# Forgetting attention, then a gelu MLP, on one core: the tail tile of v multiplied apart, the opening's normalisation reordered, and the output units of the steps spread anew

## The chip, the cores and the metric

The kernel runs on one core of one Trainium2 chip. The metric is device time in microseconds from one launch. Before the change the median of three runs is 338.88 us (338.82 to 339.25).

TensorE (PE in the profile) multiplies matrices; VectorE (DVE), ScalarE (ACT) and GpSimd (POOL) work on elements; SyncE (SP) and POOL issue the transfers of this kernel. Each engine takes its instructions in the order in which the kernel writes them.

## The reference, cut to what matters

Attention over 8 batches of 8 heads, 576 positions and head width 64, with a decay built from the running sum of log f and a causal mask; then an MLP with tanh-gelu on all 8 x 576 = 4608 tokens, 512 to 2048 to 512.

```python
scores = scale * np.matmul(q, k.transpose(0, 1, 3, 2))
log_f = np.log(np.clip(f, 0.0001, 1.0))
cum = np.cumsum(log_f, axis=-1)
decay = cum[:, :, :, None] - cum[:, :, None, :]
scores = np.where(causal, -1000000000.0, scores + decay)
attn = exp(scores - max) / (sum + 1e-09)
x = (attn @ v) as [4608, 512]
h = x @ w_in
g = 0.5 * h * (1.0 + np.tanh(c * (h + 0.044715 * h * h * h)))
return g @ w_out
```

The row's own part of the decay cancels between numerator and denominator. What is left is a weight per key, w = exp(-cum), which the kernel multiplies into v and uses again, in bf16, as the vector that gives the denominators.

## The kernel before, in words

Four heads of one batch are a *quad*; two quads make a batch, 16 quads in all. For a quad the kernel

- reorders q and k on DVE (`transpose_qk`, two instructions, line 142);
- multiplies v by the key weights into `vw` (`make_vw`, line 152). v lies in `v_nat` as five tiles of up to 128 keys. The fifth, slot `TAIL` = 4, holds the last 64 keys in its upper half, zeros in the lower. A sixth slot of `vw`, `HEAD`, repeats the first 64 keys. So `make_vw` issues two instructions: 128 x 1280 elements (five tiles of four heads of 64) and 64 x 256;
- computes scores in three rounds (`score_round`: line 170 on PE, then two exps on ACT, line 201, into `pt`), masks them on POOL (line 226);
- multiplies `pt` with the weights for the denominators (line 247, w_bf), takes reciprocals with two DVE transposes around them (lines 278 to 282), multiplies `pt` with `vw` for the outputs, two halves y = 0, 1, and scales each half into `xT` (`normalise`, line 288).

The MLP runs in chunks of 512 tokens. `mlp_in(j)` multiplies `xT` by w_in in eight pairs of psum banks, each followed by a gelu on ACT (line 329). `mlp_out(j)` is a generator: each pull emits one *unit*, one of the 16 matmuls that accumulate an output tile of 128 tokens (line 356). Four tiles of 16 units are 64 units per chunk. After the sixteenth unit DVE copies the tile out of psum (line 361) and SP stores it. A unit is one matmul with 128 columns of weights, or four with 32 columns each where the neighbours use 32 columns as well. Two psum banks (`psM`) hold the tiles.

The opening (`startup`) treats batch 0 apart. Its quads 0 and 1 use only the first 512 queries (`early_rounds`, `early_product`), which don't need the tail tile; the last 64 queries of both quads come later together (`late_scores`, `late_denominators`, `late_outputs`), and only these read slot `TAIL` of `vw`. SP loads v of quad 0 in five transfers, the tail last; POOL loads v of quad 1, then w_in in four transfers, q and k of quad 2, w_out in four, q and k of quad 3, v of batch 1. DVE's order in the opening is: transposes of quads 0 and 1, `w_bf`, `vw` of quad 0, reciprocals of quad 0, `vw` of quad 1, two normalisations of quad 0, reciprocals of quad 1, two normalisations of quad 1. The banks of the early products come from a pool of two (`psP`), so the denominators of quad 1 take the bank that the first half of quad 0's outputs had.

Then come the *steps*. `step(i, j, fill, fills)` runs three rounds r = 0, 1, 2. Each has a score round of quad i, a product of quad j (denominators, then the two halves of the outputs), and `fills[r]` units of the output of the chunk before; the transposes of the next quad, the masks and `make_vw` are placed in rounds by hand. Score banks are two pairs (tag "s"), so round r + 1 reuses the banks that the exps of round r read. In batch 0 six units are pulled first, then steps 2, 3 and 4 follow with 28, 14 and 11 units, 59 in all. The last five are drained after the first pair of the next `mlp_in`. In the batches after that two steps per batch run with units in the same way: `pull(fill, 6)`, then 26 and 27 units, again five left over.

The order is written by hand (`manual_schedule`); no planner moves anything.

Of the kernel before, what the change touches and what calls it, by code (L numbers as in the profile page):

```python
# [16 lines left out]
def kernel(  # L17
# [10 lines left out]
    nc = tc.nc  # L28

    B, H, S, D = q.shape  # L30
    BH = B * H
    NT = (S + 127) // 128
# [6 lines left out]
    NQ = BH // 4  # L39
    QPB = H // 4  # L40
# [6 lines left out]
    TAIL, HEAD = NT - 1, NT  # L47
# [25 lines left out]
    def many(n, shape, dtype, name):  # L73
        return [singles.tile(shape, dtype, name=f"{name}{i}") for i in range(n)]
# [6 lines left out]
    v_nat = many(2, [128, NT, H, D], FP32, "v_nat")  # L81
# [3 lines left out]
    vw = many(2, [128, NT + 1, 4, D], BF16, "vw")  # L85
# [8 lines left out]
    wT = singles.tile([128, NQ, NT, 4], FP32, name="wT")  # L94
# [15 lines left out]
    def load_qk(i):  # L110
        b, h0 = i // QPB, 4 * (i % QPB)
        return [nc.gpsimd.dma_start(  # L112
            out=dst[i % 2].rearrange("p a d -> p (a d)"),
            in_=src[b, h0:h0 + 4].rearrange("h (p a) d -> (h p) (a d)", p=32))
            for src, dst in ((k, k_c), (q, q_c))]
# [30 lines left out]
                    .rearrange("p (a d) -> p a d", d=D // 2),  # L146
            )

    def make_vw(i, eng=nc.gpsimd):
        h0 = 4 * (i % QPB)  # L150
        for p, n, slot in ((128, NT, 0), (64, 1, HEAD)):
            eng.tensor_mul(  # L152
                vw[i % 2][:p, slot:slot + n], v_nat[(i // QPB) % 2][:p, 0:n, h0:h0 + 4, :],
                wT[:p, i, 0:n, :].unsqueeze(3).to_broadcast([p, n, 4, D]))

    def bank_pair(tag, name):
        return pools[tag].tile([128, 2, 512], FP32, name=name, tag=tag)
# [1 line left out]
    def make_lows():  # L159
        for low, parts in zip(lows, (diag_first, diag)):  # L160
            nc.gpsimd.memset(low, 0.0)
            for p0, p1, pattern in parts:
                nc.gpsimd.affine_select(
                    out=low[p0:p1, :], in_=low[p0:p1, :], compare_op=ALU.is_ge, fill=-32768.0,
                    base=0, pattern=pattern, channel_multiplier=-1)
# [92 lines left out]
    def early_product(i, groups, ps):  # L258
        product(i, groups, ps, 0, early_parts, (0,))
        return ps  # L260
# [25 lines left out]
    def normalise(i, y, po):  # L286
        n, t0 = po.shape[-1], S * (i // QPB) % RING
        nc.vector.tensor_mul(xT[:, 2 * (i % QPB) + y, t0:t0 + n], po, rbs[i][:, 0:n])  # L288
# [87 lines left out]
    def startup():  # L376
        nc.sync.dma_start(out=f_sb, in_=f.rearrange("b h s -> (b h) s"))
        q0 = load_qk(0)[1]
        make_identity(nc, ident_f32)
        k1 = load_qk(1)[0]  # L380
        make_identity(nc, ident)
        make_lows()

        nc.vector.memset(blank, 0.0)
        warm = pools["p"].tile([128, 512], FP32, name="warm", tag="p")
        warm_up(warm, 11)
        nc.vector.memset(ones_f32, 1.0)
        nc.vector.memset(shift, -64.0)
        nc.vector.memset(wT[:128 - LAST, :, TAIL, :], 0.0)
        nc.vector.memset(w_bf[LAST:, :, HEAD, :], 0.0)  # L390
        for t_ in vw:
            nc.vector.memset(t_[LAST:, HEAD, :, :], 0.0)
        for t_ in v_nat:
            nc.vector.memset(t_[:128 - LAST, TAIL, :, :], 0.0)
        nc.vector.tensor_scalar(f_sb, f_sb, 1e-4, 1.0, op0=ALU.max, op1=ALU.min)
        nc.scalar.activation(f_sb, f_sb, AF.Ln)
        nc.vector.tensor_tensor_scan(cum_sb, ones_f32, f_sb, 0.0, op0=ALU.mult, op1=ALU.add)
        cum = pools["p"].tile([128, 512], FP32, name="small", tag="p")[:, 0:NT * BH]
        for t in range(NT):
            s0 = min(128 * t, S - 128)  # L400
            nc.tensor.transpose(cum[:, t * BH:(t + 1) * BH],
                                cum_sb[:, s0:s0 + 128], ident_f32)
        make_w(cum)
        warm_up(warm, 6)
        transpose_qk(0)
        transpose_qk(1)
        nc.vector.tensor_copy(w_bf[:, :, :NT, :], wT)
        nc.vector.tensor_copy(w_bf[:LAST, :, HEAD, :], wT[:LAST, :, 0, :])
        after(load_v(0, heads=slice(0, 4))[0], q0)
        make_vw(0, nc.vector)  # L410
        after(load_v(0, nc.gpsimd, slice(4, 8))[0], k1)
        for c in range(2):
            for u in range(QPB):
                load_w_in(c, u)
        load_qk(2)
        for c in range(4):
            load_w_out(c)
        q3 = load_qk(3)[1]
        load_v(1, nc.gpsimd, slice(0, 4))
        after(load_v(1, heads=slice(4, 8))[0], q3)  # L420

        def single(name):
            return pools["p"].tile([128, 512], FP32, name=name, tag="p")

        for r, tags, n in ((0, ("s", "s"), 4), (1, ("x", "s"), 4), (2, ("s", "x"), 2)):
            score_round(0, r, tags, True)
            warm_up(warm, n)
        score_round(1, 0, ("s", "s"), True)
        reciprocals(0, early_product(0, den_groups(0), single("po")))
        make_vw(1, nc.vector)  # L430
        score_round(1, 1, ("x", "s"), True)
        nums = [early_product(0, out_groups(0, y), single("po")) for y in range(2)]
        for y in range(2):
            normalise(0, y, nums[y])
        score_round(1, 2, ("s", "x"), True)
        late_scores()
        reciprocals(1, early_product(1, den_groups(1), single("po")))
        po = bank_pair("x", "po")
        nums = [early_product(1, out_groups(1, y), po[:, y, :]) for y in range(2)]
        phs = [bank_pair("s", "ps_h") for _ in range(2)]  # L440
        for dts in ((0, 1), (2,), (3,)):
            for ft in range(4):
                mlp_mm(0, ft, phs[ft // 2][:, ft % 2, :], dts)
            if dts[0] == 0:
                for y in range(2):
                    normalise(1, y, nums[y])
        for u in range(2):
            gelu(0, u, phs[u])
        for u in range(2, N_FT // 2):
            mlp_in(0, (u,), "x" if u % 3 == 2 else "s")  # L450
# [10 lines left out]
    def step(i, j, fill, fills):  # L461
        for r in range(3):
            if i is not None:
                score_round(i, r)
            if j is not None:
                if r == 0:
                    denominators(j)
                else:
                    attn_out(j, r - 1, "s" if i is None and r == 1 else "po")
            if (i, r) in ((2, 0), (3, 1)):  # L470
                transpose_qk(i + 1)
            if i is not None and r > 0:
                mask(i, r - 1)
            if i is not None and r == {2: 2, 3: 1}.get(i, 0):
                make_vw(i, nc.vector if i == 2 else nc.gpsimd)
            pull(fill, fills[r], 128 if j is None else 32)
            if i is not None and r == 2:
                mask(i, 2)
                if i == 2:
                    load_v(2)  # L480
                elif i < 5:
                    load_qk(i + 2)
# [9 lines left out]
    with tc.manual_schedule():  # L492
        with psum("psX", 1) as pools["x"], psum("psP", 2) as pools["p"]:
            startup()
            prepare(2)
        pools["po"] = ctx.enter_context(psum("psO", 1))
        pools["m"] = ctx.enter_context(psum("psM", 2))
        fill = none
        for b in range(B):
            if b > 0:  # L500
                mlp_in(b, (0,))
                for x in fill:
                    pass
                prepare(2 * b + 3, 2 * b + 4)
                if b + 2 < B:
                    load_v(b + 2)
                mlp_in(b, range(1, N_FT // 2))
            if b + 1 < B:

                nc.scalar.activation(scrap, shift, AF.Exp)  # L510
            fill = mlp_out(b)
            if b == 0:
                late_denominators(bank_pair("po", "po")[:, 0, :])
                pull(fill, 6, 32)
                late_outputs(bank_pair("po", "po")[:, 0, :])
                step(2, None, fill, (12, 8, 8))
                step(3, 2, fill, (4, 5, 5))
                step(4, 3, fill, (4, 4, 3))
            elif b + 1 < B:
                i = 2 * b + 3  # L520
                pull(fill, 6)
                step(i, i - 1, fill, (9, 8, 9))
                step(i + 1 if i + 1 < NQ else None, i, fill, (9, 8, 10))
        mlp_in(B, range(N_FT // 2))
        for j in (B - 1, B):
            for x in mlp_out(j):
                pass
# [30 lines left out]
```

## Time and profile before

| | |
|---|---|
| median of three runs | 338.88 us |
| the profiled execution's own time | 338.56 us |
| its span, first to last instruction | 336.9 us |
| PE busy | 328.6 us, 98% of the span |
| ACT busy | 191.3 us, 57% |
| DVE busy | 124.1 us, 37% |
| POOL busy | 115.3 us, 34% |
| granted TensorE clock | 1.000 |

A row of the timeline gives the start in us from the span's start, the length of the merged group, the engine, the line of the kernel, the operation with output and input tiles and shapes, the count, and in brackets the idle time before it with what ended it. PEld is the weight load, which overlaps the matmuls; SPq and POOLq are the engines' issuing of transfers. A group counts as busy from its first start to its last end, so a wait in its middle can hide in it. In a row on transfers the last number is the time from issue to landing.

### The profile page before, as it was taken

The page shows a single profiled execution, that of the slowest core. Times are in us where ns is not written, and L with a number is a line of the kernel's source. Part 1 is how long each engine was busy: PE and PEld are TensorE (multiplying, and loading weights), DVE is VectorE, ACT ScalarE, POOL GpSimd, SP SyncE. Part 2 cuts the span into 40 slices and gives each one's busy share as a digit, 9 for nine tenths or more (in the row PEclk, how much of TensorE's full clock was granted, in tenths as well). Part 3 has the DMA queues.
Part 4 walks back from the last instruction along what each step waited for, and adds up shares of the span by engine and source line. Part 5 has one row for each costly group of instructions (what it writes and reads, how often), then busy time and mean ns, then how long its engine had stood idle before and what let it go on. Part 6 is the DMA issues. An engine that isn't in the chain of part 4 may idle for free.

```text
span 336.9 us, 9983 instructions
## 1 busy us (share of the span) xinstructions
PE 328.6 (98%) x4513; PEld 161.0 (48%) x4535; DVE 124.1 (37%) x172; ACT 191.3 (57%) x206; POOL 115.3 (34%) x159
## 2 busy tenths in 40 slices
PE   7989999999999999999999999999999999999996
PEld 2554534444444444444478444444444454444444
DVE  7582177342526144604442342524330450000121
ACT  4876766767565757467555756576647704553000
POOL 6933248751534145242725162405520300000000
PEclk9999999999999999999999999999999999999999
DMA  7999999597107801491129310921000010000112
GB/s 130 210 188 210 220 241 204 83 221 144 66 33 156 157 33 66 95 207 44 35 71 207 73 65 33 186 57 66 34 33 0 35 64 31 2 0 27 68 69 86
DMA packets 45578, 33.29 MB, mean 99 GB/s; under 512 B 34304, under 2 KB 34560, under 8 KB 45536
## 3 DMA queue, kind: packets, MB, share of 16 engines
q0 software_dynamic: 7232, 14.81, 24.6%
q1 hardware_dynamic: 38304, 17.85, 19.9%
q8 instruction: 35, 0.57, 0.7%
q14 instruction: 7, 0.06, 0.1%
HBM read 36.85 MB, written 9.44 MB: 137 GB/s over the span
## 4 chain that ended last, share of the span: by engine, by line
PE 89%; DMA 3%; issue 3%; ACT 1%; DVE 1%; SPq 1%; POOL 1%; POOLq 0%; DVEq 0%; ACTq 0%
PE ps_h L320 37%; PE pso L356 35%; PE po L247 9%; PE ps_s L170 7%; DMA v_nat<-in_v_dram 2%; DMA q_c<-in_q_dram 1%; ACT pt L201 1%; DVE vw L152 1%; SPq L118 1%; POOL pt L226 0%; POOLq L553 0%; DVE den L278 0%; DVE xT L288 0%; POOL k_c L112 0%; DVE o_st L361 0%
## 5 line engine op out<-in xcount | busy, mean ns | idle before, releaser
L356 PE MATMUL pso<-w_out_sb,gT 128*32 128x512 bf16 (+2 forms) x1633 | 133.6, 377 | 0.5 <-issue 0.3
L320 PE MATMUL ps_h<-xT,w_in_sb 128*128 128x512 bf16 (+1 forms) x625 | 126.1, 357 | 0.9 <-issue 0.2
L201 ACT ACTIVATE pt<-ps_s 128x1024 bf16<-128x1024 f32 (+1 forms) x96 | 91.1, 1002 | 41.1 <-PE ps_s L170 37.9
L329 ACT ACTIVATE gT<-ps_h 128x1024 bf16<-128x1024 f32 (+1 forms) x81 | 74.1, 928 | 70.4 <-PE ps_h L320 69.7
L320 PEld LDWEIGHTS <-w_in_sb 128*128 128x128 bf16 x640 | 62.0, 98 | 63.5 <-issue 3.3
L356 PEld LDWEIGHTS <-gT 128*32 128x32 bf16 (+1 forms) x1639 | 59.7, 97 | 55.1 <-issue 0.8
L226 POOL TENSOR_SCALAR_AFFINE_SELECT pt<-pt 128x512 bf16<-128x512 bf16 (+1 forms) x70 | 44.1, 638 | 103.3 <-ACT pt L201 102.2
L361 DVE COPY o_st<-pso 128x512 f32<-128x512 f32 (+1 forms) x37 | 25.0, 675 | 88.0 <-PE pso L356 88.0
L278 DVE STREAM_TRANSPOSE den<-po 128x576 f32<-128x576 f32 (+2 forms) x17 | 12.7, 748 | 70.3 <-PE po L247 65.2
L152 POOL TENSOR_TENSOR vw<-v_nat,wT 128x1280 bf16<-128x1280 f32 (+1 forms) x26 | 37.7, 1471 | 0.5 <-DVE rec L280 0.4
L288 DVE TENSOR_TENSOR xT<-po,rb 128x576 bf16<-128x576 f32 (+1 forms) x32 | 23.8, 748 | 34.8 <-PE po L247 34.7
L170 PE MATMUL ps_s<-qT,kT 32*128 32x64 bf16 (+8 forms) x944 | 34.0, 286 | 1.4 <-ACT pt L201 1.1
L247 PE MATMUL po<-pt,vw 128*32 128x64 bf16 (+6 forms) x768 | 27.5, 277 | 0.0
L170 PEld LDWEIGHTS <-kT 32*128 32x128 bf16 (+1 forms) x944 | 14.7, 97 | 25.3 <-issue 21.9
L142 DVE STREAM_TRANSPOSE kT<-k_c 128x576 f32<-128x576 f32 x16 | 20.0, 1247 | 8.8 <-DMA k_c<-in_k_dram 8.8
L247 PEld LDWEIGHTS <-vw 128*32 128x32 bf16 x832 | 13.7, 96 | 13.7 <-issue 7.1
L142 DVE STREAM_TRANSPOSE qT<-q_c 128x576 f32<-128x576 f32 x16 | 19.9, 1241 | 0.8 <-DMA q_c<-in_q_dram 0.8
L112 POOL DMA_DIRECT2D k_c<-in_k_dram x16 | 9.1, 568 | 29.3 <-DVE kT L142 22.7
L247 PE MATMUL po<-pt,w_bf 128*32 128x64 bf16 (+8 forms) x384 | 14.3, 276 | 0.5 <-DVE xT L288 0.5
L282 DVE STREAM_TRANSPOSE rb<-rec 128x576 f32<-128x576 f32 (+2 forms) x17 | 12.6, 743 | 0.6
L112 POOL DMA_DIRECT2D q_c<-in_q_dram x16 | 8.7, 545 | 8.7 <-DVE qT L142 5.1
L329 ACT ACT_TABLE_LOAD x8 | 10.3, 1283 | 0.1
(43 smaller groups left out, 72.6 us busy)
## 6 DMA issues: line engine op xcount, KB each, us to landing
out_dram<-o_st SPq DMA_DIRECT2D x35, 256.0 KB, 2.1
v_nat<-in_v_dram SPq DMA_DIRECT2D x24, 256.0 KB, 6.3
k_c<-in_k_dram POOLq DMA_DIRECT2D x16, 288.0 KB, 6.1
q_c<-in_q_dram POOLq DMA_DIRECT2D x16, 288.0 KB, 7.3
w_in_sb<-in_moe_w_in_dram POOLq DMA_DIRECT2D x4, 512.0 KB, 9.8
w_out_sb<-in_moe_w_out_dram POOLq DMA_DIRECT2D x4, 512.0 KB, 17.9
v_nat<-in_v_dram SPq DMA_DIRECT2D x14, 128.0 KB, 5.6
v_nat<-in_v_dram POOLq DMA_DIRECT2D x8, 128.0 KB, 7.2
```

The lines of the kernel that those rows point to most:

```text
L112: return [nc.gpsimd.dma_start(out=dst[i % 2].rearrange("p a d -> p (a d)"), in_=src[b, h0:h0 + 4].rearrange("h (p a) d -> (h p) (a d)", p=32))
L142: nc.vector.transpose(out=dst[i % 2].rearrange("p s c -> p (s c)").bitcast(FP32) .rearrange("p (t a) -> p a t", a=S // 32), in_=src[i % 2] ...
L152: eng.tensor_mul(vw[i % 2][:p, slot:slot + n], v_nat[(i // QPB) % 2][:p, 0:n, h0:h0 + 4, :], wT[:p, i, 0:n, :].unsqueeze(3).to_broadcast([ ...
L170: nc.tensor.matmul(tiles[h // 2][m0:m0 + m, h % 2, c0:c0 + nq], kT[i % 2][32 * h:32 * h + 32, k0:k0 + m, c], qT[i % 2][32 * h:32 * h + 32, ...
L201: nc.scalar.activation(pt[i % 2][:, 2 * g:2 * g + 2, off:off + n], tiles[g][:, :, 0:n], AF.Exp, scale=scale)
L226: nc.gpsimd.affine_select(out=p[p0:p1, :, o:o + 128], in_=p[p0:p1, :, o:o + 128], compare_op=ALU.is_ge, fill=0.0, base=0, pattern=[[0, 4]] ...
L247: nc.tensor.matmul(ps[r0:r0 + w.shape[-1], o:o + nq], w, rhs[:, h, col:col + nq], start=(n in fresh), stop=(n in (0, len(parts) - 1)), ski ...
L288: nc.vector.tensor_mul(xT[:, 2 * (i % QPB) + y, t0:t0 + n], po, rbs[i][:, 0:n])
L320: nc.tensor.matmul(ph[:, o:o + m], w[:, dt], xT[:, dt, a:a + m], start=(dt == 0 and o == 0), stop=(dt == N_DT - 1), skip_group_check=True)
L329: nc.scalar.activation(gT[:, 2 * u + y:2 * u + y + n, o:o + CHUNK], ph[:, y:y + n, :], AF.Gelu_apprx_tanh)
L356: nc.tensor.matmul(ps[m:m + w, c0:c1], gT[:, ft, c + m:c + m + w], w_out_sb[:, ft, c0:c1], start=(ft == 0), stop=(ft == N_FT - 1), skip_gr ...
L361: nc.vector.tensor_copy(st[:, c0:c1], ps[:, c0:c1])
```

## The change

The diff does five things. `make_vw` takes a range of tiles; the opening calls it without the tail for both quads, and once more for the tail of each behind the normalisations of quad 1. `vw` of quad 1 is made after the normalisations of quad 0 and after the scores of its second round are written, not before. The transposes of quad 3 move from round 0 to round 1 of step 2. The units of steps 2, 3 and 4 become 26, 15 and 17, so that with the six ahead all 64 are pulled and none is left over. In the last batch that has steps, the last step takes 32 units instead of 27, again with none left over.

```diff
-    def make_vw(i, eng=nc.gpsimd):
+    def make_vw(i, eng=nc.gpsimd, t0=0, t1=NT):
         h0 = 4 * (i % QPB)
-        for p, n, slot in ((128, NT, 0), (64, 1, HEAD)):
-            eng.tensor_mul(
-                vw[i % 2][:p, slot:slot + n], v_nat[(i // QPB) % 2][:p, 0:n, h0:h0 + 4, :],
-                wT[:p, i, 0:n, :].unsqueeze(3).to_broadcast([p, n, 4, D]))
+        for p, a, z, slot in ((128, t0, t1, t0), (64, 0, 1, HEAD)):
+            if a >= t0:
+                eng.tensor_mul(
+                    vw[i % 2][:p, slot:slot + z - a],
+                    v_nat[(i // QPB) % 2][:p, a:z, h0:h0 + 4, :],
+                    wT[:p, i, a:z, :].unsqueeze(3).to_broadcast([p, z - a, 4, D]))
...
         after(load_v(0, heads=slice(0, 4))[0], q0)
-        make_vw(0, nc.vector)
+        make_vw(0, nc.vector, 0, TAIL)
...
         reciprocals(0, early_product(0, den_groups(0), single("po")))
-        make_vw(1, nc.vector)
         score_round(1, 1, ("x", "s"), True)
         nums = [early_product(0, out_groups(0, y), single("po")) for y in range(2)]
         for y in range(2):
             normalise(0, y, nums[y])
+        make_vw(1, nc.vector, 0, TAIL)
         score_round(1, 2, ("s", "x"), True)
         late_scores()
...
                 for y in range(2):
                     normalise(1, y, nums[y])
+        for i in range(QPB):
+            make_vw(i, nc.vector, TAIL)
         for u in range(2):
             gelu(0, u, phs[u])
...
-            if (i, r) in ((2, 0), (3, 1)):
+            if (i, r) in ((2, 1), (3, 1)):
                 transpose_qk(i + 1)
...
-                step(2, None, fill, (12, 8, 8))
-                step(3, 2, fill, (4, 5, 5))
-                step(4, 3, fill, (4, 4, 3))
+                step(2, None, fill, (10, 8, 8))
+                step(3, 2, fill, (4, 6, 5))
+                step(4, 3, fill, (6, 6, 5))
...
                 step(i, i - 1, fill, (9, 8, 9))
-                step(i + 1 if i + 1 < NQ else None, i, fill, (9, 8, 10))
+                if i + 1 < NQ:
+                    step(i + 1, i, fill, (9, 8, 10))
+                else:
+                    step(None, i, fill, (9, 9, 14))
```

## The prediction

> **What bounds the kernel now.** I read the page's busy line, then the order of time in the opening and in steps 2 to 4 (PE, DVE and ACT apart), then the chain of waits, then single transfers.
>
> ```profile
> span 336.9 us, 9983 instructions
> PE 328.6 (98%) x4513; PEld 161.0 (48%) x4535; DVE 124.1 (37%) x172; ACT 191.3 (57%) x206; POOL 115.3 (34%) x159
> ```
>
> PE is the bound, and an edit that only moves its work gains nothing where PE streams without a gap. It can gain where PE waits: visibly, or hidden in groups that take longer than the same group elsewhere. The change touches two such places. The first is the opening, in order of time, DVE and then PE:
>
> ```profile
> 14.89 1.82 DVE L152 TENSOR_TENSOR vw<-v_nat,wT 128x1280 bf16<-128x1280 f32 x2 [2.54 <-DMA v_nat<-in_v_dram]
> 16.63 0.70 DVE L278 STREAM_TRANSPOSE den<-po 128x512 f32<-128x512 f32 x1
> 17.65 0.71 DVE L282 STREAM_TRANSPOSE rb<-rec 128x512 f32<-128x512 f32 x1
> 18.29 1.78 DVE L152 TENSOR_TENSOR vw<-v_nat,wT 128x1280 bf16<-128x1280 f32 x2
> 19.99 1.27 DVE L288 TENSOR_TENSOR xT<-po,rb 128x512 bf16<-128x512 f32 x2
> ...
> 14.89 0.73 PE L247 MATMUL po<-pt,w_bf 128*32 128x64 bf16 x20
> ...
> 17.08 1.28 PE L247 MATMUL po<-pt,vw 128*32 128x64 bf16 x40
> ...
> 19.60 0.66 PE L170 MATMUL ps_s<-qT,kT 32*128 32x64 bf16 x62 [0.44 <-ACT pt L201]
> 20.72 0.73 PE L247 MATMUL po<-pt,w_bf 128*32 128x64 bf16 x20 [0.46 <-DVE xT L288]
> 21.26 1.28 PE L247 MATMUL po<-pt,vw 128*32 128x64 bf16 x40
> ```
>
> DVE is one queue here: vw of quad 0, the reciprocals of quad 0, vw of quad 1, the two normalisations of quad 0. PE's denominators of quad 1 need a bank that the first normalisation frees; they wait 0.46 us for it.
>
> The second place is steps 3 and 4, PE and then ACT:
>
> ```profile
> 47.14 0.91 PE L170 MATMUL ps_s<-qT,kT 32*64 32x512 bf16 x24
> 52.61 0.88 PE L170 MATMUL ps_s<-qT,kT 32*128 32x320 bf16 x16
> 58.30 0.63 PE L170 MATMUL ps_s<-qT,kT 32*128 32x64 bf16 x14 [0.25 <-ACT pt L201]
> 61.00 0.63 PE L170 MATMUL ps_s<-qT,kT 32*128 32x320 bf16 x14 [0.17 <-ACT pt L201]
> 63.00 1.90 PE L320 MATMUL ps_h<-xT,w_in_sb 128*128 128x512 bf16 x7
> 64.74 1.24 PE L356 MATMUL pso<-w_out_sb,gT 128*128 128x512 bf16 x5
> ...
> 50.87 1.94 ACT L201 ACTIVATE pt<-ps_s 128x1024 bf16<-128x1024 f32 x2 [0.76 <-PE ps_s L170]
> 53.52 1.94 ACT L201 ACTIVATE pt<-ps_s 128x1024 bf16<-128x1024 f32 x2 [0.70 <-PE ps_s L170]
> 56.31 1.94 ACT L201 ACTIVATE pt<-ps_s 128x1024 bf16<-128x1024 f32 x2 [0.86 <-PE ps_s L170]
> ...
> 63.63 1.28 ACT L329 ACT_TABLE_LOAD   x1
> 64.94 1.02 ACT L329 ACTIVATE gT<-ps_h 128x1024 bf16<-128x1024 f32 x1
> ```
>
> Each round is scores, a product, and some fill units of the out tile before. Six rounds take 47.14 to 63.00, 15.86 us. What PE itself needs for a round is seen where nothing waits, in the chain of waits of the next batch (start, length, what):
>
> ```profile
> 79.37 0.59 PE ps_s L170 x16
> ...
> 80.75 1.94 PE pso L356 x36
> 82.70 0.57 PE ps_s L170 x16
> ...
> 85.79 0.57 PE ps_s L170 x16
> ```
>
> A round with 9 units (36 matmuls) takes 82.70 - 79.37 = 3.33 us, one with 8 takes 3.09; a unit is 1.94/9 = 0.2155, so a round without units costs 1.37 to 1.39. The six rounds hold 25 units, so PE needs 6 x 1.38 + 25 x 0.2155 = 13.7 us, and 2.2 us are waits, most of them inside groups that count as busy (0.88 for scores that take 0.57 there). ACT sets the pace: its pairs of exps start 2.65 to 2.79 us apart (50.87, 53.52, 56.31), 1.94 of work and 0.7 to 0.86 from the end of the second exp through the scores that reuse its bank to the next first exp. A round of n units on PE is 1.38 + 0.2155 n: 2.24 for 4, 2.46 for 5, 2.67 for 6. Up to six units fit.
>
> **The change part by part.** *Opening.* Durations first, from the groups by form, then the chain's rows for the loads of v and the landing of the fourth of them:
>
> ```profile
> L152 DVE TENSOR_TENSOR vw<-v_nat,wT 128x1280 bf16<-128x1280 f32 x3 | 4.4, 1478 | 3.0 <-DMA v_nat<-in_v_dram 3.0
> L152 DVE TENSOR_TENSOR vw<-v_nat,wT 64x256 bf16<-64x256 f32 x3 | 1.2, 407 | 0.0
> 8.49 0.51 SPq L118
> 9.04 5.72 DMA v_nat<-in_v_dram
> v_nat<-in_v_dram SPq DMA_DIRECT2D x1, 128.0 KB, 4.5
> ```
>
> (1478 - 407)/1024 is 1.046 ns per element, so 1024 elements take 1.21 us, and the pair, which overlapped by 0.07, 1.55 instead of 1.82. Without the tail, vw of quad 0 waits for the fourth load, 8.49 + 4.5 = 12.99, not for 9.04 + 5.72 = 14.76: it runs from about 13.1 to 14.7. The reciprocals then wait for PE's denominators (14.89 + 0.73 = 15.62) and, with 1.73 as now (16.63 to 18.36), end near 17.4. The normalisations now follow at once: the first half of PE's outputs is there at 17.08 + 0.73 = 17.81, so they run 17.9 to 19.15. Then vw of quad 1, to 20.70. PE finishes the late scores at 20.26 (they still wait for ACT), starts the denominators there instead of at 20.72, and the outputs 0.54 later, at 20.80; vw of quad 1 is ready 0.1 before. Gain 0.46 us. That is the top of this term, since ACT's wait ahead of it stays; if vw of quad 0 still began at 14.89, the same sum puts vw of quad 1 at 21.0 and leaves 0.26; the bottom is 0. I take 0.46, since every term is a row of this stretch.
>
> The two tail multiplications are new: 0.41 each by the row of equal width, behind the normalisations of quad 1. DVE is idle there:
>
> ```profile
> 29.54 1.26 DVE L142 STREAM_TRANSPOSE kT<-k_c 128x576 f32<-128x576 f32 x1 [4.90 <-DMA k_c<-in_k_dram]
> ```
>
> They fit in those 4.90 us, and their reader, the late outputs, comes only behind the whole first MLP. Cost nothing; without that cover, 0.8.
>
> *What the earlier PE runs into.* The last quarter of w_out serves units 13 to 16 of the first out tile. Six units run before step 2, so it is first read by the seventh of step 2:
>
> ```profile
> 22.38 0.71 POOL L135 DMA_DIRECT2D w_out_sb<-in_moe_w_out_dram  x1 [1.81 <-DMA w_in_sb<-in_moe_w_in_dram]
> w_out_sb<-in_moe_w_out_dram POOLq DMA_DIRECT2D x1, 512.0 KB, 17.9
> 39.56 2.54 PE L356 MATMUL pso<-w_out_sb,gT 128*128 128x512 bf16 x11 [0.16 <-issue]
> ```
>
> It lands at 22.38 + 17.9 = 40.28 and is read at 39.56 + 6 x 0.2155 = 40.85 now, at 40.39 then; with 0.13 from landing to start (14.76 to 14.89 above) that is a tie. Cost 0 to 0.3, I take 0.05.
>
> *Step 2, (12,8,8) to (10,8,8).* Its later rounds are at ACT's pace too, so two units fewer in the first bring everything behind forward by 0.43. *Step 3, (4,5,5) to (4,6,5), and step 4, (4,4,3) to (6,6,5).* Seven units more. Five of them go into rounds that have room: 0 to 0.1 each for the three rounds of six, where PE's 2.67 meets ACT's 2.65; I take 0.1 in all, 0.3 is the end. The two in the last round have no exp behind them to hide under: +0.43. In return the five left over between the first and second pair of the next MLP, 5 x 0.2155 = 1.08 at 64.74, are gone. Steps together: 0.43 - 0.1 - 0.43 + 1.08 = 0.98 gained, bounds 0.78 and 1.08, and 0 if the long groups were work.
>
> What those five covered: the gelu table. All is early by 0.46 + 0.43 = 0.89 there: the load begins at 63.63 - 0.89 = 62.74 and ends at 64.02, the first pair of the MLP ends near 64.4, its gelu (1.02) near 65.6, and the third pair wants that bank near 66.1, a pair of eight matmuls (8 x 0.2155) later: 0.5 to spare. The gelu starts at 64.94, 0.03 after its load ended at 64.91, so nothing stands between them. [...]
>
> *Transposes of quad 3, a round later.* They wait for their load anyway:
>
> ```profile
> 42.43 1.26 DVE L142 STREAM_TRANSPOSE kT<-k_c 128x576 f32<-128x576 f32 x1 [3.12 <-DMA k_c<-in_k_dram]
> 43.53 1.24 DVE L142 STREAM_TRANSPOSE qT<-q_c 128x576 f32<-128x576 f32 x1
> ```
>
> They end at 44.77 in either place; step 3's first scores come at 47.14 - 0.89 = 46.25. Ahead of them DVE now copies out tile 0, which it had to hold back; behind them stand vw of quad 2, which waits for its load until 45.76 (row below), and the second copy. No DMA moves with them. Nothing gained, nothing lost. *Last batch, (9,8,10) to (9,9,14):* PE streams there at 0.2155 a unit before and after; 0.
>
> **Sum.** 0.46 - 0.05 + 0.98 = 1.4 us. The profiled execution took 338.56 us (span 336.9 and 1.66 around it) and becomes 337.16; the median shown, 338.88, stands 0.32 above it, so 337.5.
>
> **The rivals.** *Steps only, 337.9:* the late quarter of w_out, or vw of quad 1 missing its 0.1, eats the opening's gain. For it: both margins are a tenth. Against: each must miss by 0.4 to take all. *Opening only, 338.4:* PE's long groups are work, not waiting, and the fill is paid in full. Against it: the same groups take 0.57 in the next batch. *The tail is not parted, 337.7:* if the wait follows the whole tile and not its slots, vw of quad 0 still starts at 14.89; the opening gives 0.26, the sum 1.2. Against it: vw of quad 2 started when half the heads of its tile were still being issued.
>
> ```profile
> 44.80 3.37 SPq L118 DMA_DIRECT2D v_nat<-in_v_dram  x2
> ...
> 45.76 1.82 DVE L152 TENSOR_TENSOR vw<-v_nat,wT 128x1280 bf16<-128x1280 f32 x2 [0.48 <-DMA v_nat<-in_v_dram]
> ```
>
> *The gelu table uncovered, 337.7:* if a load's length again (1.28) passes before a gelu can start, the first gelu ends at 64.02 + 1.28 + 1.02 = 66.3, the third pair waits 0.2, and the sum is 1.2; the 0.03 us is against it. [...]
>
> *Slower, 339.9:* the loads on POOL's queue come one slot later. One slot is about 2.5 us (the wait of 1.81 and the issue of 0.71 in the row at 22.38). The place is unit 13 of the first out tile: PE waits there in order, and all the margin, 0.57 before, is spent by the earlier PE. From 1.4 us late it decides; one slot costs 2.45: 338.9 - 1.4 + 2.45. Against it: nothing in the opening's DMA order is changed.
>
> **How the numbers follow.** Forecast 0.60, steps only 0.13, opening only 0.09, tail not parted 0.05, table 0.03, slower 0.10. About 0.2%, 0.68 us, is what a measurement of this kernel tells from no change. The forecast, steps only, the tail and the table lie beyond it, but for some 0.06 of the weight at their weak ends: faster 0.75; opening only and those ends: same 0.15; slower 0.10. Terms at their best give 0.46 + 1.08 = 1.54, and 0.4 for what rows of one execution leave open: 336.9. The upper end reaches to opening only and a little past it, 338.7.
>
> **What would show it.** Right: vw with 1024 elements starting near 13.1, no wait for normalisation before the denominators of quad 1, the outputs of quad 1 at 20.8 and not 21.26; no out units after the next MLP's first pair, the second pair near 64.4 instead of 64.74 + 1.08 = 65.82; scores of steps 3 and 4 at ACT's pace as before. Wrong: PE waiting for w_out near 40.4, outputs of quad 1 waiting for vw near 20.8, exps of steps 3 and 4 more than 2.8 us apart, the third MLP pair waiting for a gelu.

## The result, and the profile after

| | before | after |
|---|---|---|
| median | 338.74 us (9 runs, 338.49 to 339.25) | 337.88 us (9 runs, 337.60 to 338.67) |
| the profiled execution | 338.56 us | 338.67 us |
| its span | 336.9 us | 337.0 us |

The ratio is 0.9976, 95% interval 0.9965 to 0.9986: 0.86 us faster, where 1.4 was forecast (337.5, range 336.9 to 338.7). The profiled execution of the changed kernel is the longest of its nine, and longer than the profiled one of before. That turns out to be useful: it shows the place where the executions differ.

The page of the changed kernel, busy times (PE's share fell, at a longer span):

```profile
span 337.0 us, 10056 instructions
PE 327.8 (97%) x4549; PEld 160.8 (48%) x4571; DVE 124.8 (37%) x174; ACT 191.3 (57%) x206; POOL 115.1 (34%) x159
```

Its opening in order of time, DVE and then PE:

```profile
13.19 1.55 DVE L154 TENSOR_TENSOR vw<-v_nat,wT 128x1024 bf16<-128x1024 f32 x2 [0.78 <-DMA v_nat<-in_v_dram]
17.73 1.29 DVE L291 TENSOR_TENSOR xT<-po,rb 128x512 bf16<-128x512 f32 x2 [0.43 <-PE po L250]
18.93 1.54 DVE L154 TENSOR_TENSOR vw<-v_nat,wT 128x1024 bf16<-128x1024 f32 x2
...
23.90 0.75 DVE L154 TENSOR_TENSOR vw<-v_nat,wT 128x256 bf16<-128x256 f32 x2
...
19.46 0.66 PE L173 MATMUL ps_s<-qT,kT 32*128 32x64 bf16 x62 [0.44 <-ACT pt L204]
20.05 0.73 PE L250 MATMUL po<-pt,w_bf 128*32 128x64 bf16 x20
20.61 1.26 PE L250 MATMUL po<-pt,vw 128*32 128x64 bf16 x40
21.81 1.69 PE L323 MATMUL ps_h<-xT,w_in_sb 128*128 128x512 bf16 x6
25.04 2.33 PE L323 MATMUL ps_h<-xT,w_in_sb 128*128 128x512 bf16 x10 [1.54 <-issue]
```

In this execution everything up to the first MLP is as forecast: vw waits for its own load alone, the denominators of quad 1 follow the late scores without the 0.46 us, and the MLP starts at 21.81. Then PE stands for 1.54 us, and no semaphore ended that: the profile puts it down to "issue". For comparison the first MLP before, and its first scores of step 2:

```profile
22.47 2.77 PE L320 MATMUL ps_h<-xT,w_in_sb 128*128 128x512 bf16 x11
...
38.74 0.66 PE L170 MATMUL ps_s<-qT,kT 32*64 32x512 bf16 x24
```

Before, the MLP starts 0.66 us later and runs through, so step 2 begins at 38.74; after, at 39.79 (next fence). The steps of the changed kernel, PE and then ACT:

```profile
39.79 0.66 PE L173 MATMUL ps_s<-qT,kT 32*64 32x512 bf16 x24
...
47.84 0.91 PE L173 MATMUL ps_s<-qT,kT 32*64 32x512 bf16 x24
...
56.00 0.90 PE L173 MATMUL ps_s<-qT,kT 32*64 32x512 bf16 x24
59.02 0.66 PE L173 MATMUL ps_s<-qT,kT 32*128 32x64 bf16 x16
61.70 0.67 PE L173 MATMUL ps_s<-qT,kT 32*128 32x320 bf16 x16
63.00 1.25 PE L359 MATMUL pso<-w_out_sb,gT 128*32 128x512 bf16 x20
64.18 4.06 PE L323 MATMUL ps_h<-xT,w_in_sb 128*128 128x512 bf16 x17
...
51.58 1.94 ACT L204 ACTIVATE pt<-ps_s 128x1024 bf16<-128x1024 f32 x2 [0.76 <-PE ps_s L173]
54.26 1.94 ACT L204 ACTIVATE pt<-ps_s 128x1024 bf16<-128x1024 f32 x2 [0.74 <-PE ps_s L173]
57.05 1.94 ACT L204 ACTIVATE pt<-ps_s 128x1024 bf16<-128x1024 f32 x2 [0.86 <-PE ps_s L173]
...
64.41 1.28 ACT L332 ACT_TABLE_LOAD   x1
66.12 1.02 ACT L332 ACTIVATE gT<-ps_h 128x1024 bf16<-128x1024 f32 x1 [0.43 <-PE ps_h L323]
```

The exps still start 2.68 and 2.79 us apart, so the added units cost only what lies outside ACT's pace, and the MLP's pairs follow one another (17 matmuls in one group from 64.18), where before five units stood between the first and the second. All of this comes about 1.5 us later than the prediction's clock times (second pair near 65.9 for 64.4), because step 2 began 1.05 late instead of 0.46 early.

### The profile page after: what moved, and what is told of

Same layout as the page of the kernel before. It is cut to its first block, busy times and chain, and to the rows that moved or that the text cites. A ratio compares the mean times of both kernels' runs of the same rounds, so it can differ in the third digit from the quotient of the medians.

```text
span 337.0 us, 10056 instructions
## 1 busy us (share of the span) xinstructions
PE 327.8 (97%) x4549; PEld 160.8 (48%) x4571; DVE 124.8 (37%) x174; ACT 191.3 (57%) x206; POOL 115.1 (34%) x159
## 4 chain that ended last, share of the span: by engine, by line
PE 93%; issue 2%; DVE 1%; ACT 1%; DMA 1%; POOL 0%; POOLq 0%
PE ps_h L323 37%; PE pso L359 36%; PE po L250 10%; PE ps_s L173 9%; ACT pt L204 1%; DMA f_sb<-in_f_dram 1%; PE ps_s L200 1%; PE warm L377 1%; DVE cum_sb L400 0%; POOL pt L229 0%; DVE kT L142 0%; DVE qT L142 0%; ACT f_sb L399 0%; POOLq L561 0%; DVE f_sb L398 0%
## 6 DMA issues: line engine op xcount, KB each, us to landing
w_out_sb<-in_moe_w_out_dram POOLq DMA_DIRECT2D x4, 512.0 KB, 17.8
```

## The experiments

A number that serves throughout is the profiled execution's time minus the start of its first scores of step 2: it parts what happens up to there from all that comes behind. It is 338.56 - 38.74 = 299.82 us before and 338.67 - 39.79 = 298.88 after. Behind the start of step 2 the change gains 0.94, and ahead of it, in these two executions, it loses 1.05.

**The opening alone.** The changed kernel with the old numbers of units and the transposes of quad 3 in their old round:

```diff
-            if (i, r) in ((2, 1), (3, 1)):
+            if (i, r) in ((2, 0), (3, 1)):
...
-                step(2, None, fill, (10, 8, 8))
-                step(3, 2, fill, (4, 6, 5))
-                step(4, 3, fill, (6, 6, 5))
+                step(2, None, fill, (12, 8, 8))
+                step(3, 2, fill, (4, 5, 5))
+                step(4, 3, fill, (4, 4, 3))
...
-                    step(None, i, fill, (9, 9, 14))
+                    step(None, i, fill, (9, 8, 10))
```

> The changed kernel with the old units in the steps and the transposes in their old place; only the opening's edits are left. Theory A (the profile of the changed kernel shows PE standing 1.5 us before the eighth matmul of the first MLP, where no semaphore is waited for; PE has run out of instructions there, the refill comes when it comes, and the 0.46 us that the opening gains are spent in that wait): the time of before, within 0.3 us (338.4 to 339.0), and a gap at the same matmul. Theory B (the opening pays its 0.46, the steps pay less than reckoned): 0.4 to 0.5 us faster than before. Theory C (the second load of w_in lands late): a gap too, but at the third quarter of the weights, the ninth matmul, where the wait for that load stands.

339.15 us against 338.91 on the same chip, ratio 1.0007 (0.9994 to 1.0019): at most 0.2 us gained (0.0006 x 338.91), so the 0.46 is excluded. PE in order of time:

```profile
21.91 1.69 PE L323 MATMUL ps_h<-xT,w_in_sb 128*128 128x512 bf16 x7
23.79 1.04 PE L323 MATMUL ps_h<-xT,w_in_sb 128*128 128x512 bf16 x4 [0.19 <-issue]
...
38.54 0.66 PE L173 MATMUL ps_s<-qT,kT 32*64 32x512 bf16 x24
```

The MLP starts 0.56 us earlier than before and step 2 only 0.20: the "issue" gap is there, shorter.

**The steps alone.** The kernel before with the new numbers of units in steps 2 to 4, and nothing else:

```diff
-                step(2, None, fill, (12, 8, 8))
-                step(3, 2, fill, (4, 5, 5))
-                step(4, 3, fill, (4, 4, 3))
+                step(2, None, fill, (10, 8, 8))
+                step(3, 2, fill, (4, 6, 5))
+                step(4, 3, fill, (6, 6, 5))
```

> The kernel before with only the units of steps 2, 3 and 4 spread anew; opening, transposes and the last batch as before. Theory A: nearly all of the measured gain is here, 0.85 to 1.0 us faster than before. Theory B: 0.4 us faster. Scores of steps 3 and 4 start 2.65 to 2.8 us apart in both.

337.74 us against the same 338.91, ratio 0.9968 (0.9957 to 0.9978): all of the change's gain, without its opening, its transposes and its last batch. PE:

```profile
21.94 1.69 PE L320 MATMUL ps_h<-xT,w_in_sb 128*128 128x512 bf16 x7
23.85 1.04 PE L320 MATMUL ps_h<-xT,w_in_sb 128*128 128x512 bf16 x4 [0.22 <-issue]
...
38.60 0.66 PE L170 MATMUL ps_s<-qT,kT 32*64 32x512 bf16 x24
...
41.00 1.02 PE L356 MATMUL pso<-w_out_sb,gT 128*128 128x512 bf16 x4 [0.33 <-DMA w_out_sb<-in_moe_w_out_dram]
```

Two things were not expected. The old opening, too, reaches the MLP at 21.94 in this execution: v's tail had landed earlier (vw of quad 0 starts at 14.35, not 14.89), and the wait for the normalisation was gone. And the gap ends at 23.85, 0.06 from where it ends in the kernel with the new opening. From the end of the gap to step 2 it is 38.60 - 23.85 = 14.75 us here, 38.54 - 23.79 = 14.75 in the opening alone, and 39.79 - 25.04 = 14.75 in the changed kernel. So the end of this gap sets the start of step 2, and not the start of the MLP. The gap costs a little more than its idle time: from the MLP's start to step 2 it is 16.27 us in the first trace of before, and 16.63, 16.66 and 17.98 in the opening alone, the steps alone and the changed kernel, 0.36 to 1.71 more for gaps of 0.19 to 1.54. PE waited besides for the last quarter of w_out.

**What ends the gap.** PE's recorded instructions counted up to the gap (702 weight loads and matmuls, and three of its sequencer near the start) give 705 in each of these kernels (703 in the changed one, whose page has 4549 matmuls beside 4571 weight loads, so that some records seem to be missing). The theory formed here, which no row shows as such: PE's instructions come in pieces, and it had run out. The DMA view of the changed kernel from 22.6 to 23.6 us (queue: packets, MB, share of 16 engines):

```profile
q0 software_dynamic: 100, 0.19, 104.3%
q8 instruction: 1, 0.02, 5.6%
```

In that microsecond one packet crossed the instruction queue between 100 of the loads, whose share of the 16 engines was 104.3%. Two kernels test it by moving the count against the work, with warm-up matmuls, matmuls on zeros that no result depends on and that all come ahead of the gap.

**Fewer warm-ups.** Eight of the changed kernel's 27 warm-up matmuls out, 16 instructions:

```diff
-        warm_up(warm, 6)
+        warm_up(warm, 4)
...
-        for r, tags, n in ((0, ("s", "s"), 4), (1, ("x", "s"), 4), (2, ("s", "x"), 2)):
+        for r, tags, n in ((0, ("s", "s"), 2), (1, ("x", "s"), 2), (2, ("s", "x"), 0)):
```

> The changed kernel with 8 of the 27 warm-up matmuls taken out (16 PE instructions, none of which any result depends on). Theory A: PE runs out 16 instructions later in the program, by which time the refill has come; no gap in the first MLP, about 0.5 us faster than the changed kernel, 337.2 to 337.5. Theories B and C: the gap is not a matter of the number of instructions, so the time of the changed kernel, and the gap at the same matmul. If the clock falls because PE idles more, the granted clock shows it.

**More warm-ups.** Four of the six replaced by twelve of 64 columns, 16 instructions more:

```diff
-            nc.tensor.matmul(ps, blank[:, 0:128], blank, start=True, stop=True)
+            nc.tensor.matmul(ps, blank[:, 0:128], blank[:, 0:ps.shape[-1]], start=True, stop=True)
...
-        warm_up(warm, 6)
+        warm_up(warm, 2)
+        warm_up(warm[:, 0:64], 12)
```

> The changed kernel with 8 pairs of PE instructions more: four of the six long warm-up matmuls become twelve short ones of 64 columns. Theory A: PE runs out 16 instructions earlier, within the outputs of quad 1 or at their end, and waits 1 to 1.5 us longer than the changed kernel: 338.9 to 339.5. Theories B and C: within 0.3 us of the changed kernel.

337.73 us (ratio 0.9968, 0.9959 to 0.9978) with fewer, 340.14 (1.0038, 1.0022 to 1.0054) with more. Both times missed what was expected: with fewer the gap did not vanish, and with more a second one came. PE's gaps with fewer:

```profile
25.64 10.75 PE L323 MATMUL ps_h<-xT,w_in_sb 128*128 128x512 bf16 x49 [0.24 <-issue]
```

and with more:

```profile
23.94 0.28 PE L250 MATMUL po<-pt,vw 128*32 128x256 bf16 x1 [1.61 <-issue]
...
44.59 0.37 PE L173 MATMUL ps_s<-qT,kT 32*128 32x448 bf16 x3 [0.68 <-issue]
```

The gap moved with the count: 8 pairs of load and matmul further into the MLP with 16 instructions fewer (49 matmuls are left behind it instead of 57), and back into the outputs of quad 1 with 16 more. It has no ties to an operation, a tile or a bank. A second one appeared at the count 1217, 512 after 705. The records of packets on the instruction queue, beside PE's counts, for the kernels told of so far and below:

```
kernel              PE count   PE passes the    packet          PE goes on
                    at gap     count 256 less   from     to
before               -            19.60         21.58  22.55    23.85 (load held 0.07)
before, 2nd trace   705           19.61         22.02  22.92    24.50
opening only        705           19.56         21.49  22.44    23.79
steps only          705           19.55         21.52  22.50    23.85
changed             703           19.47         22.63  23.52    25.04
changed, 2nd trace  705           19.70         21.55  22.49    23.91
fewer warm-ups      705           19.70         23.18  24.07    25.64
more warm-ups       705           18.74         21.71  22.65    23.94
more warm-ups      1217           39.47         42.08  43.05    44.59
changed, fp32       449           14.66         19.23  20.18    21.52
changed, fp32       705           21.52         25.69  26.64    27.98
fp32, 8, 9, 9       449           14.45         19.45  20.41    21.84
fp32, 8, 9, 9       705           21.84         25.86  26.75    28.32
16 out, without q   449           15.62         19.84  20.79    22.20
```

In every row PE goes on 1.3 to 1.6 us after the packet's end, and the packet starts 1.9 to 5.0 us after PE has passed the count that lies 256 lower. The pages of before and of the changed kernel give 35 packets on this queue and 0.57 MB, 16 KB each. The author's reading, which these rows fit: PE stands there because the instructions behind the count are not there yet, and the packet brings them; what a packet holds, and what makes it start when it does, was not shown. In this stretch PE goes through 256 instructions in some 4.2 us (19.60 to 23.85 before), in short late scores (62 in 0.66 us), denominators (20 in 0.73) and outputs (40 in 1.28); from the count passed to going on it takes 4.2 to 6.5 us in the rows with 705. What the opening gains lies behind the count 449, which PE passes at 19.47 to 19.70 in the first six rows, with either opening. PE comes to 705 earlier for it, but the packet starts at much the same time or later: at 21.49, 21.55 and 22.63 with the new opening, at 21.52, 21.58 and 22.02 with the old one. The idle time in PE's rows marked "issue" at these counts is 0.15 to 1.61 us.

**The changed kernel again**, unchanged, for a second trace:

> The changed kernel once more, for a second trace and for its time beside the next three on the same chip. Theory A: a gap at the same matmul of the first MLP, anywhere between 0 and 1.5 us long, and 337.7 to 338.0.

337.93 us, ratio 0.9974 (0.9962 to 0.9986). PE:

```profile
22.04 1.69 PE L323 MATMUL ps_h<-xT,w_in_sb 128*128 128x512 bf16 x7
23.91 12.48 PE L323 MATMUL ps_h<-xT,w_in_sb 128*128 128x512 bf16 x57 [0.18 <-issue]
```

Its profiled execution took 337.51 us, 1.16 less than the first one; the gap ends 1.13 earlier, 14.75 before step 2 at 38.66. So these two executions differ by the gap. The packet alone is not shown to be the reason, though, since a second limit stood right behind it in the first trace (POOL, then the time from issue to landing):

```profile
23.95 0.71 POOL L135 DMA_DIRECT2D w_out_sb<-in_moe_w_out_dram  x1 [1.78 <-DMA w_in_sb<-in_moe_w_in_dram]
w_out_sb<-in_moe_w_out_dram POOLq DMA_DIRECT2D x2, 512.0 KB, 17.8
```

The last quarter of w_out lands there at 23.95 + 17.8 = 41.7, and the seventh unit of step 2, which reads it, starts at 41.77. In the second trace it was issued at 22.31, and the seventh unit starts at 40.56. With the packet on time and w_out as late, PE would by these rows have stood at the seventh unit instead, for much the same loss. Packet and load are both late in the first trace and both on time in the second. 337.51 - 38.66 = 298.85 repeats the steps' number.

**Sixteen warm-ups out**, in the changed kernel, in the steps alone, and in the changed kernel that besides does not load q of quad 2, whose scores then rest on stale data; the aim was to move the gap out of the first MLP and to see w_out alone:

```diff
-        warm_up(warm, 11)
+        warm_up(warm, 7)
...
-        warm_up(warm, 6)
+        warm_up(warm, 4)
...
-        for r, tags, n in ((0, ("s", "s"), 4), (1, ("x", "s"), 4), (2, ("s", "x"), 2)):
+        for r, tags, n in ((0, ("s", "s"), 0), (1, ("x", "s"), 0), (2, ("s", "x"), 0)):
```

> The changed kernel with 16 of the 27 warm-up matmuls taken out (32 PE instructions). Theory A: PE needs the refill three microseconds later than in the changed kernel, so no gap in the first MLP; what the opening gains then meets the last quarter of w_out near 40.9, so only some of the 0.46 shows: 337.3 to 337.7. Theory B (the opening pays, no matter of the refill): as the changed kernel, 337.9. If the granted clock falls early, the time rises instead and the clock says so.

> The opening of before with the new units in steps 2 to 4, and the same 16 warm-up matmuls out: against after_16 this shows the opening alone with the refill out of the way. Theory A with w_out as the next limit: within 0.2 us of after_16. If the opening's 0.46 is worth anything once the refill is gone: 0.3 to 0.46 slower than after_16.

> after_16 with the load of q of quad 2 left out (its place in the buffer keeps quad 0's q, so the results of quad 2 are not the reference's); 288 KB fewer stand ahead of w_out. If w_out is what holds the earlier PE near 40.9, it now lands some 1.3 us sooner, PE doesn't wait there, and the time falls by 0.3 to 0.5 against after_16. If not, no difference.

339.87 us (1.0041, 1.0023 to 1.0058), 339.66 (1.0023, 1.0012 to 1.0034) and 339.84 (1.0035, 1.0022 to 1.0048): all slower than before, and a miss. Windows of the first (stretch: length, busy times, granted clock, DMA share, GB/s), and the same 24 scores there and in the changed kernel:

```profile
12.00:16.00 4.00, 3.33 (x43) 1.46 (x40) 1.63 (x3) 2.98 (x4) 4.00 (x8) 0.60 1.10 196
16.00:20.00 4.00, 4.00 (x67) 2.10 (x69) 1.68 (x3) 2.93 (x4) 2.17 (x5) 0.55 1.01 143
...
14.11 1.61 PE L173 MATMUL ps_s<-qT,kT 32*64 32x512 bf16 x24
```

```profile
13.53 0.97 PE L173 MATMUL ps_s<-qT,kT 32*64 32x512 bf16 x24
```

The 24 scores take 1.61 instead of 0.97 us. PE was busy for 2.26 us of the four from 4 to 8 (3.78 in the changed kernel's second trace). From 12 to 20 us the granted clock was 0.60 and 0.55, as above, where the changed kernel has 1.00; it was 1.00 in the second all the while, and 0.50 from 8 to 16 in the third. The opening lost more than 2 us (MLP at 24.34, 25.00 and 24.41). The gap was gone from the first MLP, as expected, but nothing can be read of w_out. Behind the start of step 2 they take 298.79, 298.82 and 298.83 us (340.09 - 41.27 for the second, with the old opening): the steps' gain once more.

**Fewer instructions at full clock.** The 27 warm-ups replaced by 8 in fp32, which keep PE busy (1.08 us for one with 512 columns) with fewer instructions (22 recorded ones fewer, not the 48 that were expected, since each of the 8 is recorded as two loads and two matmuls); in the changed kernel, in the steps alone, and in the changed kernel with step 2, and no other step, spread 8, 9, 9:

```diff
-    blank = singles.tile([128, 512], BF16, name="blank")
+    blank = singles.tile([128, 512], FP32, name="blank")
...
-        warm_up(warm, 11)
+        warm_up(warm, 3)
...
-        warm_up(warm, 6)
+        warm_up(warm, 1)
+        warm_up(warm[:, 0:256], 1)
...
-        for r, tags, n in ((0, ("s", "s"), 4), (1, ("x", "s"), 4), (2, ("s", "x"), 2)):
+        for r, tags, n in ((0, ("s", "s"), 512), (1, ("x", "s"), 512), (2, ("s", "x"), 256)):
...
-            warm_up(warm, n)
+            warm_up(warm[:, 0:n], 1)
```

> The changed kernel with its 27 bf16 warm-up matmuls replaced by 8 longer fp32 ones, so that TensorE is kept as busy and issues 48 instructions fewer before the first MLP; nothing else differs. Theory A (TensorE's instructions run out at a fixed count and the next piece lands late): the gap in the ninth pair of the first MLP is gone from there and lies after it, in the second pairs or none; the first scores of step 2 begin at 38.2 to 38.4 us instead of 38.66, unless the last quarter of w_out (landed at 40.3 to 41.75 in the other traces) holds the last accumulation by up to 0.5; time 337.4 to 337.6. Theory B (the opening's gain is limited by w_out alone, or was never there): time as the changed kernel, 337.9, whether the gap moves or not. If the granted clock falls in the opening the run tells nothing of either.

> The opening of the kernel before with the steps spread anew, and the same 8 fp32 warm-ups. Theory A: without the gap the opening before reaches the first scores of step 2 at 38.5 or so, and the difference to the changed opening with the same warm-ups is what the opening is worth once the refill is out of the way: 0 (tail of v lands early) to 0.46 us. Theory B: 337.7 to 337.9, no difference to the changed opening.

> The changed kernel with the fp32 warm-ups and with step 2 of the first two batches spread 8, 9, 9 instead of 10, 8, 8. If scores of rounds 3 and 4 wait for no exponential any more with 8 pieces ahead of them, up to 0.2 us faster than with 10, 8, 8; if the cover was needed, 0.1 to 0.4 slower, with an idle time of TensorE behind ScalarE at the second scores of step 2.

338.39 us (0.9986, 0.9971 to 1.0), 337.79 (0.9971, 0.9955 to 0.9988) and 338.31 (0.9978, 0.9954 to 1.0003), against 339.01. The granted clock was 1.0 in the profiled executions of all three. PE in the steps alone with these warm-ups:

```profile
21.88 2.98 PE L320 MATMUL ps_h<-xT,w_in_sb 128*128 128x512 bf16 x13
...
38.14 0.66 PE L170 MATMUL ps_s<-qT,kT 32*64 32x512 bf16 x24
...
40.54 1.02 PE L356 MATMUL pso<-w_out_sb,gT 128*128 128x512 bf16 x4 [0.33 <-DMA w_out_sb<-in_moe_w_out_dram]
```

Without the gap step 2 begins at 38.14, the earliest of all traces, 0.6 ahead of before, and with the *old* opening. The next in line is w_out: PE stands idle 0.33 for its last quarter, step 2 takes 46.60 - 38.14 = 8.46 us instead of the 7.98 of the changed kernel's second trace, and the time behind the start of step 2 rises to 337.65 - 38.14 = 299.51. The median is near that of the steps alone (337.74). In the changed kernel the same edit went wrong (POOL's issues first, then PE):

```profile
12.97 2.80 POOL L131 DMA_DIRECT2D w_in_sb<-in_moe_w_in_dram  x4
...
21.52 0.57 PE L173 MATMUL ps_s<-qT,kT 32*128 32x64 bf16 x50 [1.01 <-issue]
...
27.98 10.10 PE L323 MATMUL ps_h<-xT,w_in_sb 128*128 128x512 bf16 x46 [0.15 <-issue]
...
40.36 0.66 PE L173 MATMUL ps_s<-qT,kT 32*64 32x512 bf16 x24
```

The gap at 705 moved 11 pairs on, as 22 instructions fewer should make it, but an earlier one, at the count 449, opened in the late scores, with 1.01 us here and 1.55 with 8, 9, 9. So the 38.2 to 38.4 expected for step 2 was missed by 2 us. PE passed the count 193 at 14.66 and 14.45 us in these two, and the packet then started at 19.23 and 19.45; where it passed that count by 14.04, in nine other traces, the packet started by 16.05, and where it passed it at 15.05 to 16.09, with 16 warm-ups out, the packet started at 19.77 to 20.39. In between the loads of w_in join in (POOL issues them from 12.97 to 15.77); that they hold the packet back was not shown. PE came late to that count because its first fp32 warm-ups, three records from 4.24 on, took 2.77 and 2.76 us in these two executions and 1.87 in the steps alone; why they did is open. Behind the start of step 2, 8, 9, 9 takes 339.42 - 40.69 = 298.73 against 339.15 - 40.36 = 298.79: not told apart, so this spread has no more to give here.

**The kernel before, a second trace:**

> The kernel before, unchanged, for a second trace. If the 0.46 us wait for the normalisation at the sums of quad 1 is usual, it is there again with v's tail landing near 14.8 us; if it hangs on the landing, the tail lands near 14.2 and the wait is under 0.2. The ninth pair of the first MLP is held for instructions only if the piece lands after 23.5 us.

```profile
20.39 0.73 PE L247 MATMUL po<-pt,w_bf 128*32 128x64 bf16 x20
20.93 1.28 PE L247 MATMUL po<-pt,vw 128*32 128x64 bf16 x40
22.15 1.69 PE L320 MATMUL ps_h<-xT,w_in_sb 128*128 128x512 bf16 x7
...
24.50 0.39 PE L320 MATMUL ps_h<-xT,w_in_sb 128*128 128x512 bf16 x1 [0.67 <-issue]
...
39.25 0.66 PE L170 MATMUL ps_s<-qT,kT 32*64 32x512 bf16 x24
```

The wait for the normalisation, 0.46 in the first trace, is no longer shown as one (the late scores end at 20.27, the denominators start at 20.39; vw of quad 0 starts at 14.56), and the gap of 0.67 is here in the kernel before as well. 339.12 - 39.25 = 299.87.

## Why the prediction was right and where it was wrong

| executions | MLP starts | step 2 starts | time behind it |
|---|---|---|---|
| before, two traces | 22.47, 22.15 | 38.74, 39.25 | 299.82, 299.87 |
| opening only | 21.91 | 38.54 | 299.90 |
| steps only | 21.94 | 38.60 | 299.43 (w_out's wait in it) |
| changed, two traces | 21.81, 22.04 | 39.79, 38.66 | 298.88, 298.85 |

The time, 337.88, lies in the forecast's range, and the faster kernel was forecast; but the sum was not met. Of its three terms the steps' came true and the opening's, a third of the gain, brought nothing. The measured time is that of the rival "steps only", 337.9, which had a chance of 0.13. That it still falls near the forecast is in part luck: the one term that held was the larger one.

- **Steps, 0.98: right.** 299.8 to 299.9 with the old numbers of units against 298.7 to 298.9 with the new ones where w_out costs less than 0.1, 0.9 to 1.1. The terms too: from the first scores of step 2 to those of step 3 8.40 us before (47.14 - 38.74) and 8.05 after (7.98 in the second trace), 0.35 to 0.42 for the 0.43; steps 3 and 4 take 16.34 (64.18 - 47.84) instead of 15.86, 0.48 lost for the 0.53; the rest, 0.94 - 0.35 + 0.48 = 1.07, lies behind the start of the next MLP, where the units left over are gone, for 1.08. Seven units more are 7 x 0.2155 = 1.51 us of PE's work, and steps 3 and 4 grew by 0.48: the rest went into waits, so the long groups were waits.
- **The opening, 0.46: the step that failed.** The mechanism came true row by row (vw at 13.19 for 13.1, normalisations at 17.73 for 17.9, outputs at 20.61 for 20.8), and the two tail multiplications took 0.75 under cover. But "PE starts earlier" was carried straight through to the sum, as if nothing but w_out and vw stood between. What stands there is the gap at the count 705, by the author's reading PE's own supply of instructions: PE goes on 1.3 to 1.6 us after the packet's end, and step 2 starts 14.75 us later in three kernels, so what the opening gains ahead of that is waited away. This wait is in no row of the trace of before, and yet that trace bounds it. The packet ended at 22.55, and the weight load with 703 records ahead of it, as the load behind the gap in the changed kernel has them, started at 23.85, held for 0.07, with its matmul at 24.00. Where PE is held for longer, the matmul starts 0.01 after that load (25.03 and 25.04 in the changed kernel). So with this packet an earlier PE could, by an estimate from these rows, have gained 0.14 us at most, not 0.46.
- **The price of 0.46 was also that of one execution.** Of the four traces of the old opening at full clock it is there in one. With v's tail landing earlier the old opening reaches the MLP at 21.88, 21.94 and 22.15, the new one at 21.81 to 22.04 (where no gap lies ahead of the MLP).
- **w_out, 0.05: right for the changed kernel, its bound too low.** Step 2 takes 8.05 us in the first trace of the changed kernel and 7.98 in the second, so at most 0.1 is lost there. Where PE reaches w_out earlier against its landing, it takes 8.20 (fewer warm-ups) and 8.46 (steps alone, both forms): 0.2 and 0.5 lost, where 0.3 was the upper bound and PE's idle time shows 0.33.
- **The gelu table: no wait.** The load starts at 64.41, 0.02 after the last exp ends (64.39), and ends at 65.69; the gelu starts at 66.12 behind PE's 0.43, and the third pair follows without a gap. A gelu one more load's length (1.28) after the load's end would have started at 66.97.
- **Transposes and the last batch, 0: right.** The steps alone have neither, and are no slower; with 16 warm-ups out the time behind the start of step 2 is 298.82 without them and 298.79 with them.
- **The rivals.** In amount "steps only, 337.9" came true, by a mechanism that it didn't name. What "slower" names, w_out some microseconds late, is seen in single executions, with either opening: the last quarter was issued at 23.95 in the first trace of the changed kernel and at 23.83 in that of the steps alone, 1.5 us later than the 22.38 before, but at 22.31 in the changed kernel's second trace. It cost the steps alone 0.5, not 2.45; in the changed kernel's first trace the gap hid it.

What stays open: whether the opening gains anything once the gap at 705 and w_out are both out of the way, and what makes a packet, or the last load of w_out, late in one execution and not in the next. None of the versions tried is told apart from the changed kernel on the fast side (337.73 to 337.93 for four of them).

## What to carry to other kernels

A gain in an opening was worth here only what the next things that didn't move with it let through: the last load of w_out, and a packet on the instruction queue, at whose end plus 1.3 to 1.6 us PE went on. So list, for the engine that bounds the kernel, not only its data and banks but also the rows of that queue, above all behind a stretch of many short instructions (256 in some 4.2 us here) and while large loads run (DMA share 1.11 from 19 to 24 us before). Where a gap is marked "issue", count the engine's instructions up to it in two kernels: here it stayed at the count and not at the operation. And a wait of half a microsecond that hangs on a transfer should be read from two executions before it is put in a sum.

## What the runs showed of the hardware

- PE stood idle at the counts 449, 705 and 1217, for 0.15 to 1.61 us in the rows marked "issue", and went on 1.3 to 1.6 us after the end of a packet on the instruction queue. The pages of before and of the changed kernel show 35 such packets, 16 KB each. That they bring PE's next instructions is the author's reading.
- With 16 of the 27 warm-up matmuls out of the changed kernel the granted clock was 0.60 and 0.55 from 12 to 20 us, against 1.00, and the MLP started at 24.34 instead of 21.81 and 22.04. In the steps alone with the same 16 out the column of the granted clock shows 1.00, and yet the same 24 scores take 1.62 us, against 0.97 in the changed kernel, as the row has it:

```profile
15.15 1.62 PE L170 MATMUL ps_s<-qT,kT 32*64 32x512 bf16 x24
```
